# Second feed-forward product issued over 256 weight columns per matmul instead of 512, into the halves of the same accumulator

## The chip, the core and the metric

One core of one Trainium2 chip runs the whole program. Its engines work side by side: TensorE (matmuls, PE in the profile, with its weight loads shown apart as PEld), VectorE (DVE), ScalarE (ACT), GpSimd (POOL) and the queues that issue DMA transfers. The metric is the device time of one execution in microseconds (us); lower is better. A matmul here multiplies a stationary block (loaded first, by an instruction of its own, LDWEIGHTS) with a moving block that streams through the array column by column; the sums land in PSUM, the accumulator memory.

## What is computed

The reference is an attention in two parts followed by a gated feed-forward network:

```python
# q, k, v: (8, 8, 576, 64); factor 4
out_d = sm_attn(mean4(q), mean4(k), mean4(v))      # coarse attention on 144 tokens
out_local = softmax(where(|i - j| < 4, q k / 8)) v # band of 7 neighbours
x = (repeat4(out_d) + out_local) as (4608, 512)
xn = x / sqrt(mean(x * x) + 1e-6) * rms_g
g, val = xn @ w_gate, xn @ w_val                   # (4608, 1536)
out = (g * sigmoid(g) * val) @ w_out               # (4608, 512)
```

## The kernel before

The 4608 tokens are worked on in 18 chunks of 256 tokens (`NCH`, `C`). For every chunk the kernel computes the banded attention on VectorE and ScalarE, adds the coarse attention, normalizes, turns the result with TensorE transposes (line 1080) so that the model dimension lies on partitions, and runs the feed-forward network on TensorE.

Each float32 operand of the two large products is split into a high part and a low part, and each product is made of three: high by high, and high by low in both directions. `Forward.first` (matmul on line 1445) does the first product: for each of 12 slices of 128 hidden units, for gate and for value, 12 matmuls of 128x128 weights as the stationary block with 256 tokens as the moving block, all into one half of a PSUM tile. `Forward.second` (matmul on line 1487) does the second product: for each of the 12 hidden slices `f` and each half `j` of the chunk's tokens, three matmuls with 128x128 hidden activations as the stationary block (`hh`, the high part, twice; `hl`, the low part, once) and 512 columns of `w_out` as the moving block, into the PSUM tile `o[j]` of 128x512, one whole bank. That makes 18 * 12 * 2 * 3 = 1296 matmuls on line 1487.

Between the two, for a pair of slices `n`, ScalarE and VectorE compute the gate: `tanh` (L1453), `gate` (L1457), `product` (L1462), `high` (L1468, writes `hh`) and `low` (L1471, writes `hl`). The second product of a pair runs one pair late (`LAG`), so that TensorE has a first product to do while the gate is computed.

The first three chunks are ordered by a planner (`Plan`) that gives each step an engine, a cost and a due time; it plans one call of `second` (six matmuls) at 1.375 us. From chunk 3 on the loop at the end orders the work: per pair, 24 matmuls of gate and 24 of value (48 on line 1445), then two calls of `second`, with small matmuls of the coarse attention (scores L630, transposes L660, values L675), of the next chunk's mean (L1057) and its transposes (L1080) placed between them. TensorE's order there is fixed by a chain: `in_line` makes each matmul follow the one before it. On the other engines the framework's scheduler chooses the order. When a chunk's twelve slices are summed, `copy` (L740) takes `o[j]` out of PSUM and `store` (L1506) writes it to memory.

Of the kernel before, what the change touches and what calls it, by code (L numbers as in the profile page):

```python
# [27 lines left out]
DM, DF = H * D, 1536  # L28
KT = DM // P
NF = DF // P  # L30
# [200 lines left out]
def attn_moe_kernel(  # L231
# [16 lines left out]
    nc = tc.nc  # L248
# [240 lines left out]
    def heat(out, fresh=True):  # L489

        n = plan.idle
        if spare["open"] and made:
            if "tile" not in spare:
                spare["tile"] = ps_o.tile([P, DM], FP32, name="ps_o")
            out, fresh, n = spare["tile"], True, plan.gap
        n, plan.idle, plan.gap = n * WARM_SHARE, 0.0, 0.0
        cols = 1
        for d in out.shape[1:]:
            cols *= d
        if len(out.shape) > 2:  # L500
            out = out.rearrange({3: "p a b -> p (a b)", 4: "p a b c -> p (a b c)"}[len(out.shape)])
        cols = min(cols, 4 * P) // P * P
        for _ in range(int(n * 2400 / cols) if n > WARM_LEAST and made else 0):
            nc.tensor.matmul(
                out=out[:, :cols], lhsT=one_sb[:, :out.shape[0]], rhs=bcast(zero_sb, 1, cols // zero_sb.shape[1]), start=fresh, stop=fresh,
                skip_group_check=not fresh,
            )
# [6 lines left out]
    def in_line(make):  # L514

        with tc.issue_after(line["last"]) if line["last"] else nullcontext():
            done = make()
        if line["last"]:
            line["last"] = done.ins
        return done  # L520
# [839 lines left out]
    class Forward:  # L1360
# [116 lines left out]
        def second(self, n, i, js=range(2)):  # L1477
            f = 2 * n + i
            if f == 0:
                self.o = [ps_o.tile([P, DM], FP32, name="ps_o") for _ in range(2)]  # L1480
            heat(self.o[0], fresh=f == 0)
            hh, hl = self.hs[n][:, 0, i], self.hs[n][:, 1, i]
            w = [x.part(f // 4)[:, f % 4] for x in wo]
            for j in js:
                cols = slice(j * P, (j + 1) * P)
                for m, (lhs, rhs) in enumerate(((hh, w[0]), (hh, w[1]), (hl, w[0]))):
                    in_line(lambda: nc.tensor.matmul(  # L1487
                        out=self.o[j], lhsT=lhs[:, cols], rhs=rhs,
                        start=(f == 0 and m == 0), stop=(f == NF - 1 and m == 2),
                    ))  # L1490

        def copy(self, j, parts=1):
            if j == 0:
# [16 lines left out]
    for fg in range(3):  # L1510
# [3 lines left out]
        for f in range(4 * fg, 4 * fg + 4, 2 if fg < 2 else 1):  # L1514
            m = 2 if fg < 2 else 1
# [234 lines left out]
```

## Time and profile before

| what | value |
|---|---|
| median of 3 runs | 1086.33 us (1085.03 to 1090.29) |
| span of the profiled execution | 1085.7 us |
| TensorE matmul, busy | 1056.4 us, 97% of the span |
| TensorE weight load, busy | 958.9 us, 88% |
| VectorE, busy | 915.9 us, 84% |
| ScalarE, busy | 598.4 us, 55% |
| GpSimd, busy | 162.0 us, 15% |

The profiled execution lies 0.6 us under the median of the timed runs. Busy time of a matmul includes its way through the array, which overlaps the next matmul; what one matmul costs in a dense stream is therefore read as the distance between the starts of two of them, not as its duration. In a timeline, consecutive instructions of one kind stand in one row with their count.

### The profile page before, as it was taken

How to read it: one execution, taken by the hardware profiler on the slowest of the kernel's cores; microseconds unless marked ns; L12 is line 12 of the kernel's file. 1: busy time of each engine (PE TensorE's matmuls, PEld its weight loads, DVE VectorE, ACT ScalarE, POOL GpSimd, SP SyncE). 2: the span in 40 equal slices, each digit the busy share in tenths (PEclk: the TensorE clock that was granted, in tenths of full speed). 3: DMA queues.
4: the chain of work that ended last, by engine and by line, in shares of the span. 5: the costliest groups of instructions: out<-in, count | busy, mean ns of one | idle time of the engine just before them, and what ended most of it. 6: DMA issues, size and time to landing. Idle time of an engine off the chain costs nothing.

```text
span 1085.7 us, 21625 instructions
## 1 busy us (share of the span) xinstructions
PE 1056.4 (97%) x7983; PEld 958.9 (88%) x7983; DVE 915.9 (84%) x1556; ACT 598.4 (55%) x2029; POOL 162.0 (15%) x200
## 2 busy tenths in 40 slices
PE   6889999999999999999999999999999999999998
PEld 3559899898988999999999999999999989899997
DVE  7789999798969998989898989898989898985322
ACT  5776565737366556565656556565646464554121
POOL 6544654301210000000001000000000000000000
PEclk9899999999999999999999999999999999999999
DMA  9875657323644443434344444442222231300000
GB/s 287 301 216 168 164 142 164 81 80 87 141 98 104 105 129 86 130 85 117 86 99 109 112 98 103 111 103 78 76 73 71 74 96 46 104 17 20 1 20 20
DMA packets 79181, 114.08 MB, mean 105 GB/s; under 512 B 33038, under 2 KB 40406, under 8 KB 79076
## 3 DMA queue, kind: packets, MB, share of 16 engines
q1 hardware_dynamic: 48116, 88.11, 26.5%
q0 software_dynamic: 11680, 19.78, 11.5%
q10 hardware_dynamic: 19280, 4.82, 2.0%
q8 instruction: 62, 1.02, 0.4%
q14 instruction: 43, 0.35, 0.1%
HBM read 100.86 MB, written 11.80 MB: 104 GB/s over the span
## 4 chain that ended last, share of the span: by engine, by line
PE 72%; DVE 6%; ACT 3%; DMA 3%; issue 2%; POOL 0%; SPq 0%; ACTq 0%; DVEq 0%; POOLq 0%
PE ps_h L1445 43%; PE ps_o L1487 22%; PE ps_a L675 2%; ACT prod L1010 2%; DVE x_t L1027 2%; DVE prod L964 1%; DMA qk<-in_qk_sum_dram 1%; PE ps_a L630 1%; PE ps_a L660 1%; PE ps_a L1080 1%; DVE sc L968 1%; DVE prod L1017 1%; DMA kv<-in_k_pad_dram 1%; DVE hs L1471 0%; DVE sil L1462 0%
## 5 line engine op out<-in xcount | busy, mean ns | idle before, releaser
L1445 PE MATMUL ps_h<-xh,w 128*128 128x256 f32 x3456 | 619.9, 279 | 0.1
L1445 PEld LDWEIGHTS ps_h<-xh,w 128*128 128x128 f32 x3456 | 532.3, 188 | 9.0 <-issue 4.5
L1445 PE MATMUL ps_h<-xl,w 128*128 128x256 f32 x1728 | 479.5, 278 | 0.0
L1487 PE MATMUL ps_o<-wo,hs 128*128 128x512 f32 x1296 | 329.3, 396 | 8.4 <-DVE hs L1471 6.2
L1445 PEld LDWEIGHTS ps_h<-xl,w 128*128 128x128 f32 x1728 | 324.9, 188 | 4.3 <-issue 0.6
L1487 PEld LDWEIGHTS ps_o<-wo,hs 128*128 128x128 f32 x1296 | 231.5, 188 | 54.1 <-DVE hs L1471 9.4
L1010 ACT ACTIVATE prod<-kv,sc 128x64 f32<-128x64 f32 x1024 | 263.0, 407 | 25.6 <-DVE sc L1001 8.0
L1468 ACT ACTIVATE hs<-sil 128x512 fp32r<-128x512 f32 x108 | 68.1, 631 | 165.4 <-DVE sil L1462 133.1
L964 DVE TENSOR_TENSOR prod<-q_t,kv 128x896 f32<-128x896 f32 x128 | 138.7, 1104 | 4.6 <-DMA q_t<-in_q_band_dram 3.6
L1027 DVE TENSOR_REDUCE x_t<-prod 128x128 f32<-128x896 f32 x128 | 134.5, 1077 | 3.2 <-ACT prod L1010 3.1
L968 DVE TENSOR_REDUCE sc<-prod 128x14 f32<-128x896 f32 x128 | 135.4, 1075 | 0.2
L1453 ACT ACTIVATE sil<-ps_h 128x512 f32<-128x512 f32 x108 | 64.3, 596 | 125.2 <-PE ps_h L1445 114.6
L1457 DVE SCALAR_TENSOR_TENSOR sil<-sil,ps_h 128x512 f32<-128x512 f32 x108 | 73.6, 682 | 53.9 <-ACT sil L1453 53.1
L1017 DVE TENSOR_TENSOR prod<-sc,kv 128x384 f32<-128x384 f32 (+1 forms) x128 | 106.2, 866 | 0.2
L1462 DVE SCALAR_TENSOR_TENSOR sil<-sil,ps_h 128x512 f32<-128x512 f32 x108 | 73.9, 685 | 35.2 <-PE ps_h L1445 34.9
L1471 DVE TENSOR_TENSOR hs<-sil,hs 128x512 fp32r<-128x512 f32 x102 | 70.1, 688 | 20.1 <-ACT hs L1468 20.0
L417 POOL DMA_DIRECT2D qk<-in_qk_sum_dram x42 | 39.0, 928 | 237.1 <-DMA qk<-in_qk_sum_dram 171.5
L417 POOL DMA_DIRECT2D vs<-in_v_sum_dram x42 | 38.0, 904 | 228.0 <-DMA vs<-in_v_sum_dram 183.4
L650 ACT ACTIVATE a_g<-ps_a,m_g 72x144 f32<-72x144 f32 x128 | 46.5, 371 | 43.0 <-DVE m_g L645 26.2
L1050 ACT ACTIVATE up_t<-x_t 128x128 f32<-128x128 f32 x128 | 39.1, 305 | 11.2 <-DVE x_t L1040 7.0
L675 PEld LDWEIGHTS ps_a<-vs,a_g 72*72 72x72 f32 x512 | 37.9, 145 | 5.4 <-issue 0.8
L740 ACT COPY a_g<-ps_a 72x288 f32<-72x288 f32 x56 | 20.1, 396 | 37.9 <-PE ps_a L660 37.8
(155 smaller groups left out, 815.0 us busy)
## 6 DMA issues: line engine op xcount, KB each, us to landing
kv<-in_k_pad_dram SPq DMA_DIRECT2D x56, 320.0 KB
kv<-in_v_pad_dram SPq DMA_DIRECT2D x56, 320.0 KB
qk<-in_qk_sum_dram POOLq DMA_DIRECT2D x42, 288.0 KB, 4.4
out_dram<-o_sb SPq DMA_DIRECT2D x92, 72.0 KB
vs<-in_v_sum_dram POOLq DMA_DIRECT2D x42, 144.0 KB, 3.9
q_t<-in_q_band_dram SPq DMA_DIRECT2D x150, 36.0 KB
w<-in_w_gate_dram SPq DMA_DIRECT2D x8, 512.0 KB
w<-in_w_val_dram SPq DMA_DIRECT2D x8, 512.0 KB
```

The lines of the kernel that those rows point to most:

```text
L417: nc.gpsimd.dma_start(out=t, in_=(qk_sum, v_sum)[i][self.b, j, :, self.half], accum_op=ALU.add)
L964: nc.vector.tensor_tensor(out=pr, in0=bcast(q[:, s0:s0 + 2], 2, NO), in1=window(k, s0), op=ALU.mult)
L968: nc.vector.tensor_reduce(out=self.sc[:, j, par, s0:s0 + 2], in_=self.pr[i], axis=AX.X, op=ALU.add,)
L1010: nc.scalar.activation(out=self.pr[i][:, o, s], in_=self.v[j, par][:, s0 + s + o], func=AF.Copy, scale=p[:, s, o:o + 1],)
L1017: (nc.vector if engine == "DVE" else nc.gpsimd).tensor_tensor(out=self.pr[i][:, a:b], in0=bcast(p[:, :, a:b].rearrange("p s o -> p o s"), ...
L1027: nc.vector.tensor_reduce(out=self.x[j][:, s0:s0 + 2, par], in_=pr.rearrange("p o s d -> p s d o"), axis=AX.X, op=ALU.add,)
L1445: self.last = nc.tensor.matmul(out=p[n][:, i], lhsT=wi[:, k], rhs=xi[:, k], start=(m == 0), stop=(m == 3 * KT - 1),).ins
L1457: nc.vector.scalar_tensor_tensor(out=self.sil[n], in0=self.sil[n], scalar=1.0, in1=self.g[n], op0=ALU.add, op1=ALU.mult,)
L1462: nc.vector.scalar_tensor_tensor(out=self.sil[n], in0=self.sil[n], scalar=0.5, in1=self.v[n], op0=ALU.mult, op1=ALU.mult,)
L1468: nc.scalar.activation(out=self.hs[n][:, 0], in_=self.sil[n], func=AF.Copy)
L1471: low["last"] = (nc.gpsimd if engine == "POOL" else nc.vector).tensor_tensor(out=self.hs[n][:, 1], in0=self.sil[n], in1=self.hs[n][:, 0], ...
L1487: in_line(lambda: nc.tensor.matmul(out=self.o[j], lhsT=lhs[:, cols], rhs=rhs, start=(f == 0 and m == 0), stop=(f == NF - 1 and m == 2),))
```

## The change

For every hidden slice, token half and product part, the one matmul over 512 columns of `w_out` becomes two over 256 columns each, with the same stationary block, into the left and the right half of the same PSUM tile. Only the first matmul of a chunk's accumulation (`f == 0`, `m == 0`) stays whole. Per chunk 2 of 72 matmuls stay and 70 are split; over 18 chunks 36 stay and 1260 become 2520. The same columns are streamed in all, and the same sums are formed in the same order.

```diff
                 for m, (lhs, rhs) in enumerate(((hh, w[0]), (hh, w[1]), (hl, w[0]))):
-                    in_line(lambda: nc.tensor.matmul(
-                        out=self.o[j], lhsT=lhs[:, cols], rhs=rhs,
-                        start=(f == 0 and m == 0), stop=(f == NF - 1 and m == 2),
-                    ))
+                    parts = 1 if m == 0 and f == 0 else 2
+                    for h in range(parts):
+                        part = slice(h * DM // parts, (h + 1) * DM // parts)
+                        in_line(lambda: nc.tensor.matmul(
+                            out=self.o[j][:, part], lhsT=lhs[:, cols], rhs=rhs[:, part],
+                            start=(f == 0 and m == 0), stop=(f == NF - 1 and m == 2 and h == parts - 1),
+                        ))
```

## Rows read from the trace of the kernel before

**Rows 1.** Page: busy us (share, instructions), granted TensorE clock in 40 slices

```profile
PE 1056.4 (97%) x7983; PEld 958.9 (88%) x7983; DVE 915.9 (84%) x1556; ACT 598.4 (55%) x2029; POOL 162.0 (15%) x200
PEclk9899999999999999999999999999999999999999
```

**Rows 2.** Page: chain that ended last, shares of the span by engine

```profile
PE 72%; DVE 6%; ACT 3%; DMA 3%; issue 2%; POOL 0%; SPq 0%; ACTq 0%; DVEq 0%; POOLq 0%
```

**Rows 3.** Page, costliest groups: busy, mean ns of one, idle before and releaser

```profile
L1487 PE MATMUL ps_o<-wo,hs 128*128 128x512 f32 x1296 | 329.3, 396 | 8.4 <-DVE hs L1471 6.2
```

**Rows 4.** Groups of TensorE matmuls by line, from 360 us to the end

```profile
L1445 PE MATMUL ps_h<-xh,w 128*128 128x256 f32 x2560 | 452.6, 277 | 0.0
L1445 PE MATMUL ps_h<-xl,w 128*128 128x256 f32 x1280 | 354.1, 277 | 0.0
L1487 PE MATMUL ps_o<-wo,hs 128*128 128x512 f32 x972 | 244.4, 395 | 3.6 <-DVE hs L1471 3.6
```

**Rows 5.** Timeline of PE, 600 to 606 us: start us, us, instruction

```profile
600.15 0.28 PE L1445 MATMUL ps_h<-xh,w 128*128 128x256 f32 x1
...
601.30 0.28 PE L1445 MATMUL ps_h<-xl,w 128*128 128x256 f32 x1
...
605.38 0.28 PE L1445 MATMUL ps_h<-xl,w 128*128 128x256 f32 x1
...
605.61 0.62 PE L1487 MATMUL ps_o<-wo,hs 128*128 128x512 f32 x2
```

**Rows 6.** Timeline of PE, 716 to 727 us: a stretch of line 1487

```profile
716.10 2.91 PE L1487 MATMUL ps_o<-wo,hs 128*128 128x512 f32 x12
718.85 1.20 PE L675 MATMUL ps_a<-vs,a_g 72*72 72x64 f32 x16
```

**Rows 7.** Timeline of PEld, 716 to 720 us: the weight loads of that stretch

```profile
715.99 2.59 PEld L1487 LDWEIGHTS ps_o<-wo,hs 128*128 128x128 f32 x12
```

**Rows 8.** Timeline of PE, 847 to 862 us: slow stretch, then quick

```profile
847.66 0.29 PE L1057 MATMUL ps_a<-ss,same_sb 128*128 128x8 f32 x2
...
848.00 0.28 PE L1445 MATMUL ps_h<-xl,w 128*128 128x256 f32 x1
...
853.54 2.96 PE L1487 MATMUL ps_o<-wo,hs 128*128 128x512 f32 x12
856.34 0.28 PE L1445 MATMUL ps_h<-xh,w 128*128 128x256 f32 x1
...
861.80 0.39 PE L1487 MATMUL ps_o<-wo,hs 128*128 128x512 f32 x1
```

**Rows 9.** Timeline of PE, 204 to 222 us: a long slow stretch of line 1445

```profile
204.52 0.28 PE L1445 MATMUL ps_h<-xl,w 128*128 128x256 f32 x1
...
221.84 0.28 PE L1445 MATMUL ps_h<-xl,w 128*128 128x256 f32 x1
```

**Rows 10.** Timeline of PE, 331 to 338 us: line 1445 after line 630

```profile
332.41 0.28 PE L1445 MATMUL ps_h<-xl,w 128*128 128x256 f32 x1
...
337.94 0.40 PE L1487 MATMUL ps_o<-wo,hs 128*128 128x512 f32 x1
```

**Rows 11.** Timeline of PE, 360 to 367 us: line 1445 after line 630

```profile
361.40 0.29 PE L1445 MATMUL ps_h<-xl,w 128*128 128x256 f32 x1
...
366.75 0.62 PE L1487 MATMUL ps_o<-wo,hs 128*128 128x512 f32 x2
```

**Rows 12.** Timeline of PE, 356 to 420 us: small matmuls between

```profile
368.12 1.04 PE L1080 MATMUL ps_a<-ident_sb,x_t 128*128 128x128 f32 x8
...
377.22 0.67 PE L660 MATMUL ps_a<-ident_sb,a_g 72*72 72x72 f32 x8
...
387.37 1.19 PE L675 MATMUL ps_a<-vs,a_g 72*72 72x64 f32 x16
...
404.29 0.66 PE L660 MATMUL ps_a<-ident_sb,a_g 72*72 72x72 f32 x8
...
414.66 1.20 PE L675 MATMUL ps_a<-vs,a_g 72*72 72x64 f32 x16
```

## The prediction

> **What bounds the kernel now.** I read the busy shares first: TensorE is busy for 97% of the span, every other engine for less, and the granted clock is nine tenths or more of the upper level, 2.4 GHz, in every slice of 40 from the third on [rows 1]. In the chain that ended last TensorE has 72%, VectorE 6% [rows 2]. So a nanosecond on TensorE counts nearly in full, unless TensorE was waiting anyway. Does it wait on the changed line? Over the whole run line 1487 had 8.4 us of idle time before it, 6.2 of them for `hl` of VectorE [rows 3]; from 360 us to the end it is 3.6 us, and no other line of TensorE waits there [rows 4]. The change is therefore priced by the pace of TensorE's stream, and the durations of 279 and 396 ns are no help, since they overlap. I take the distance of starts.
>
> **What one piece costs, quick pace.** Line 1445 is what the new matmul looks like: 128x128 stationary, 256 moving columns, into half of a bank, one weight load each. 48 of them run from 600.15 to 605.61, 113.8 ns each; the 36 from 601.30 to 605.38 take 113.3 ns each [rows 5]. The 12 whole ones of line 1487 from 716.10 to 718.85 take 229.2 ns each [rows 6]. Two pieces at 113.3 are 226.7 ns, 2.5 ns less than one whole. From 360 us on there are 972 matmuls on line 1487 [rows 4]; 2 of 72 stay whole, 945 are split: 945 * 2.5 = 2.4 us less.
>
> A smaller term: the 48 of rows 5 cost 5.46 us where 48 at 113.3 would be 5.44. The first few matmuls of line 1445 after line 1487 are slower before they settle. If that comes from the change of length between the two lines, it goes; 3840 matmuls [rows 4] are 80 such stretches of 48, at 0.02 us 1.6 us. I count it in the best case, bound zero to 1.6.
>
> **The additional weight loads.** 1260 are added. TensorE issues one load per matmul, 7983 of each [rows 1], though `hh` is stationary twice running, so none is left out. Before, one load had 229 ns of streaming to hide in; now 113. The load starts 0.11 us ahead of its matmul [rows 6, 7]. Line 1445 has exactly this ratio and keeps 113.3 ns, so I cost the loads at nothing beyond what is in that pace. If they were not covered, the price would be in the pace of the pieces, and that is the next part.
>
> The Trainium skill, "TensorE: Matmul & The Clock Gate", section "Back-to-back issue gap", speaks against the change: a gap of N/2.4 ns plus about 2.5 ns per matmul, so each split would cost 2.5 ns. By that rule 1260 splits would add an estimated 3.2 us. The trace disagrees so far: the pieces of rows 5 are shorter than half a whole one of rows 6, not longer.
>
> **The slow pace.** The same code has a second pace. From 204.52 to 221.84 there are 147 matmuls of line 1445, 117.8 ns each [rows 9]; from 848.00 to 853.54 there are 47 at 117.9, and the 12 whole ones behind them take 233.3 ns each [rows 8]. The granted clock shows no difference between the stages of the one and of the other [rows 1]. So it is 4.4 ns more for 256 columns and 4 ns more for 512; two slow pieces (235.5) cost 2 ns more than one slow whole. The pace sticks: nothing in these 147 steps ends it. It is chosen where the stream starts anew behind other matmuls: behind line 630 it was 117.7 ns once (332.41 to 337.94, 47 steps) [rows 10] and 113.8 another time (361.40 to 366.75) [rows 11]; behind line 1057 it was slow [rows 8]. And it is left at a stretch of line 1487: the 48 matmuls from 856.34 to 861.80 are back at 113.8 [rows 8]. I read the alternation of 512 and 256 columns as what shakes the stream out of the slow pace. The change takes this away: from the first to the second product the step would be the same, and a slow pace could run on until the next other matmul.
>
> From 360 us on there will be 3840 matmuls on line 1445 and 1890 pieces, 5730 steps; all of them slow would cost 5730 * 4.4 = 25 us. How many? In a pattern of some 55 us that repeats, three groups of small matmuls (at 368.12, 377.22, 404.29) stand between two calls of `second`, where 512 columns now follow and soon 256 will; two groups (387.37, 414.66, and then line 630) stand before line 1445 and don't change what follows them [rows 12]. The stretches behind the three are 9.1, 10.2 and, up to 414.66, 10.4 us, 0.54 of the pattern. Behind such groups (lines 660 and 1057) the trace has nine places where 256 columns follow directly; four went slow, one of them shown [rows 8]. So 0.54 * 4/9 = 0.24 of the steps: 6.0 us more. The bounds are none (0 us) and all behind those three, 0.54: 13.5 us.
>
> Before 360 us there are 324 matmuls on line 1487, 315 to be split, in a stage where both paces occur: by 2.5 less or 2 more each that is -0.8 to +0.6 us, and I take zero.
>
> **What hides nothing or stays.** The wait for `hl` comes after two matmuls per `j` as before, with the last piece of `hh` ending some nanoseconds earlier; a shift of this size moves the 3.6 us of waits by no more than their own size. If TensorE becomes quicker, VectorE (84%) is late next, in those same waits. `in_line` fixes TensorE's order, so the pieces stand where the whole stood; nothing is moved past a queue and no wait or DMA is added. `copy` waits for the last piece instead of the last whole. The scheduler may order VectorE's and ScalarE's work differently, since it sees more instructions; its price is bounded by the waits that are there, some 4 us either way.
>
> **Sum.** Quick pieces -2.4, settling -1.6, slow stretches +6.0, early stage 0: +2.0 us. The profiled execution, 1085.7, would be 1087.7; the median lies 0.6 above it, at 1086.3. Forecast 1088.3 us, rounded to 1088.
>
> **Rivals.**
> - All quick. The pieces take the quick pace everywhere after 360 us, as line 1445 mostly does now: -4.0 us, 1082.3. For it: behind line 630 the quick pace returns again and again [rows 11]; against it: rows 8 to 10. Chance 0.25.
> - Slow for long (the other side). Without 512 columns nothing ends the slow pace, and it runs through both products. Slower than 0.5% (5.4 us) means that the slow share passes (5.4 + 4.0)/25 = 0.38; at 0.54 it is -4.0 + 13.5 = +9.5, 1096. Since the pattern repeats, a group that starts slow once may do so in every chunk. Chance 0.20.
> - A fixed cost for each issued matmul, the rule named above. With one half nanosecond more than the quick pace for every piece, 2520 * 0.5 = 1.3 us; with the 2.5 ns of a difference that rows 5 and 6 show, turned the other way, 1260 * 2.5 = 3.2 us, 1089.5. Against it: rows 5. Chance 0.05.
> - Another order on VectorE or ScalarE: waits of line 1487 grow or go, 1083 to 1092. For it: DVE at 84%; against it: TensorE's fixed order. Chance 0.10.
> - That the change doesn't do what it says would show as 1296 matmuls on the line; as every matmul gets its own load now, I see no way to it.
>
> **How the numbers follow.** The mixed case has 0.40, the others 0.25, 0.20, 0.05 and 0.10. The range goes from 1082 (all quick) to 1096 (slow behind all three groups); outside are a still slower pace, an early stage that gains too, and part of the last rival, less than 2 in 10. About 0.5% (5.4 us) is what a measurement of this kernel can tell from no change. Faster by more than that needs all quick and a gain before 360 us as well (0.05) or a better order (0.03): 0.08. Slower by more: the slow rival 0.20, the upper end of the mixed case 0.06, a worse order 0.03: 0.29. The rest, 0.63, is the same.
>
> **What would show it.** Right: 2556 matmuls on line 1487 (36 of 512 columns), pieces at 113 or 118 ns and nothing else, stretches at 118 that begin behind lines 660, 1057 or 1080 and run on through both products. All quick: 113.3 throughout after 360 us, with no settling at the head of line 1445. Wrong: pieces well above 118 ns (loads not covered), idle time before line 1487 well above 4 us after 360 us, or a lower granted clock.

## The result, and the profile after

| | kernel before | changed kernel |
|---|---|---|
| median of the runs | 1086.57 us (1085.03 to 1090.29) | 1095.28 us (1094.03 to 1096.96) |
| span of the profiled execution | 1085.7 us | 1095.2 us |
| ratio after to before | | 1.0072, 95% interval 1.0052 to 1.0091 |

The change makes the kernel slower by 0.72%, more than the 0.5% bound. The page of the changed kernel (busy us, share and instructions of each engine; the chain that ended last; the group of the changed line, now line 1490) answers to [rows 1 to 3]:

```profile
PE 1068.9 (98%) x9243; PEld 1028.3 (94%) x9243; DVE 913.7 (83%) x1556; ACT 597.0 (55%) x2029; POOL 159.7 (15%) x200
...
PE 79%; DVE 9%; ACT 4%; DMA 4%; issue 2%; POOL 1%; SPq 1%; ACTq 0%; DVEq 0%; POOLq 0%
...
L1490 PE MATMUL ps_o<-wo,hs 128*128 128x256 f32 (+1 forms) x2556 | 333.7, 282 | 5.1 <-DVE hs L1471 4.5
```

TensorE's busy time rose from 1056.4 to 1068.9 us and its share of the chain from 72 to 79%; all other engines kept theirs. Idle time before the changed line fell, from 8.4 to 5.1 us. So nothing new is waited for: TensorE's own stream got longer. The groups of its matmuls from 360 us to the end (busy, mean ns of one, idle before) answer to [rows 4]:

```profile
L1445 PE MATMUL ps_h<-xh,w 128*128 128x256 f32 x2560 | 457.9, 279 | 0.0
L1445 PE MATMUL ps_h<-xl,w 128*128 128x256 f32 x1280 | 356.1, 278 | 0.0
L1490 PE MATMUL ps_o<-wo,hs 128*128 128x256 f32 x1933 | 249.3, 281 | 2.8 <-DVE hs L1471 2.7
```

1933 matmuls stand on the changed line where there were 972. But look at line 1445, which the change doesn't touch: its first row went from 452.6 to 457.9 us busy and from 277 to 279 ns, its second from 354.1 to 356.1.

Where the 9.5 us of the profiled executions came in, by the starts of the same matmul of line 1445 in both traces: at the 1297th (351.21 us before, 353.25 after) the distance is 2.0 us; from there to the last one of the 5184 it grows by 7.3 us, evenly, some 0.3 us in every 28; 0.2 us come behind it.

The even growth can be seen in a timeline of PE near the end (start us, us, engine, line, tile, shape, count):

```profile
1059.52 2.88 PE L1490 MATMUL ps_o<-wo,hs 128*128 128x256 f32 x24
1062.24 0.28 PE L1445 MATMUL ps_h<-xh,w 128*128 128x256 f32 x1
...
1067.90 2.99 PE L1490 MATMUL ps_o<-wo,hs 128*128 128x256 f32 x24
1070.73 0.28 PE L1445 MATMUL ps_h<-xh,w 128*128 128x256 f32 x1
```

and further on:

```profile
1076.18 2.88 PE L1490 MATMUL ps_o<-wo,hs 128*128 128x256 f32 x24
1078.90 0.28 PE L1445 MATMUL ps_h<-xh,w 128*128 128x256 f32 x1
...
1084.56 5.70 PE L1490 MATMUL ps_o<-wo,hs 128*128 128x256 f32 x47
```

A piece is one of the two 256-column matmuls that a whole one became. Read the distances between the rows. The 24 pieces from 1059.52 to 1062.24 take 113.3 ns each; the 48 of line 1445 behind them, to 1067.90, 117.9; the next 24 pieces 117.9 (2.83 us); the next 48 of line 1445 113.5 (5.45 us); then pieces at 113.3 (2.72 us) and line 1445 at 117.9 again (5.66 us). Both paces of [rows 5, 8 and 9] are there and nothing else, but here they alternate: slow in line 1445 and the pieces behind it, quick in the next, through both products. In the kernel before, the 48 after such a stretch took 5.46 us [rows 5, 8].

What else differs between a slow and a quick stretch of line 1445 there? Two windows (us, busy time of PE, PEld, DVE, ACT, POOL with counts, granted clock, DMA share, GB/s), the slow one first:

```profile
1062.24:1067.90 5.66, 5.66 (x51) 5.66 (x49) 0.69 (x1) 0.60 (x1) 0.00 (x0) 1.00 0.00 0
1070.73:1076.18 5.45, 5.45 (x50) 5.45 (x49) 0.69 (x1) 0.60 (x1) 0.00 (x0) 1.00 0.00 0
```

Nothing that these views show: the granted clock is 1.00 in both, the DMA share is zero, and VectorE and ScalarE are busy for the same 0.69 and 0.60 us. So the clock and the DMA traffic are out as causes of the slow pace here.

From the starts of all neighbouring matmuls after 360 us (pairs with a wait between them left out) the mean step of line 1445 is 115.26 ns after and 113.86 before; 41% of the steps are at 116 ns or more, where there were 10%. The pieces have 116.34 ns, 65% of them slow; the wholes had 229.38. So line 1445 costs 1.40 * 3818 = 5.3 us more, the changed line (2 * 116.34 - 229.38) * 1815/2 = 3.0 us more, and its waits are 0.8 us less (2.8 us idle after 360 us against 3.6): 7.5 us, where 7.3 are measured. Of the steps at 116 ns or more, the 10% of before are mostly the first few of each stretch; of its 80 stretches of line 1445 after 360 us only 2 are slow as a whole, and 31 in the change.

### The profile page after: what moved, and what is told of

It is laid out like the page before. It is cut to its first block, busy times and chain, and to the rows that moved or that the text cites. A ratio compares the mean times of both kernels' runs of the same rounds, so it can differ in the third digit from the quotient of the medians.

```text
span 1095.2 us, 24157 instructions
## 1 busy us (share of the span) xinstructions
PE 1068.9 (98%) x9243; PEld 1028.3 (94%) x9243; DVE 913.7 (83%) x1556; ACT 597.0 (55%) x2029; POOL 159.7 (15%) x200
## 4 chain that ended last, share of the span: by engine, by line
PE 79%; DVE 9%; ACT 4%; DMA 4%; issue 2%; POOL 1%; SPq 1%; ACTq 0%; DVEq 0%; POOLq 0%
PE ps_h L1445 47%; PE ps_o L1490 24%; ACT prod L1010 3%; PE ps_a L675 2%; DMA w<-in_w_val_dram 1%; DVE prod L964 1%; DVE x_t L1027 1%; PE ps_a L630 1%; PE ps_a L1080 1%; PE ps_a L660 1%; DVE sc L968 1%; DMA kv<-in_k_pad_dram 1%; DMA q_t<-in_q_band_dram 1%; DVE prod L1017 1%; DVE sil L1462 1%
## 5 line engine op out<-in xcount | busy, mean ns | idle before, releaser
L1445 PE MATMUL ps_h<-xh,w 128*128 128x256 f32 x3456 | 627.0, 280 | 0.0
L1490 PE MATMUL ps_o<-wo,hs 128*128 128x256 f32 (+1 forms) x2556 | 333.7, 282 | 5.1 <-DVE hs L1471 4.5
L1490 PEld LDWEIGHTS ps_o<-wo,hs 128*128 128x128 f32 x2556 | 311.8, 188 | 9.3 <-DVE hs L1471 6.0
L675 PE MATMUL ps_a<-vs,a_g 72*72 72x64 f32 x512 | 39.9, 231 | 0.8 <-DVE vs L481 0.4
```

Source lines behind the costliest of these rows:

```text
L1445: self.last = nc.tensor.matmul(out=p[n][:, i], lhsT=wi[:, k], rhs=xi[:, k], start=(m == 0), stop=(m == 3 * KT - 1),).ins
L1490: in_line(lambda: nc.tensor.matmul(out=self.o[j][:, part], lhsT=lhs[:, cols], rhs=rhs[:, part], start=(f == 0 and m == 0), stop=(f == NF - ...
```

## The experiments

The two theories are named as in the expectations. **Load theory**: each split costs something of its own (a load without cover, a fixed cost of a matmul), wherever it stands. **Pace theory**: a piece costs no more than half a whole one; what costs is the slow pace, and line 1445 pays most of it. **Order theory**: another order of the other engines makes TensorE wait. A stretch is a row of matmuls of one line and length; it is called slow when the median of its steps is 116 ns or more (for wholes, above 231 ns). A joint is the place where one stretch follows another. The kernels differ from the one before in the condition that leaves a matmul of line 1487 whole, written `parts = 1 if f == 0 and m == 0 or ... else 2` with the additional condition in place of the dots, unless something else is shown; the diffs stand against the changed kernel's line for `parts`. All times "after 360 us" are from the 1297th to the last matmul of line 1445 in the profiled execution, one for each kernel; steps and stretches are counted from 360 us on, a step under the line that it starts from. Ratios are to the kernel before, timed beside each, with their 95% interval.

| kernel | ratio | splits, of 1260 | after 360 us | step of line 1445, ns | piece, ns | slow stretches of line 1445, of 80 |
|---|---|---|---|---|---|---|
| before | | 0 | 723.9 us | 113.86 | | 2 |
| the change | 1.0072 (1.0052 to 1.0091) | 1260 | 731.2 | 115.26 | 116.34 | 31 |
| late only | 1.0074 (1.0056 to 1.0092) | 980 | 731.1 | 115.26 | 116.36 | 31 |
| early only | 0.9989 (0.9970 to 1.0009) | 280 | 724.4 | 113.95 | | 4 |
| first of a pair whole | 1.0098 (1.0078 to 1.0117) | 1170 | 734.7 | 115.98 | 117.52 | 45 |
| last of a pair whole | 1.0082 (1.0060 to 1.0103) | 1152 | 731.3 | 115.30 | 116.28 | 32 |
| turned order, no split | 1.0000 (0.9986 to 1.0013) | 0 | 724.4 | 113.96 | | 4 |
| turned order, the change | 1.0054 (1.0025 to 1.0083) | 1260 | 731.2 | 115.26 | 116.36 | 31 |
| last of a pair split | 1.0066 (1.0043 to 1.0089) | 108 | 729.3 | 115.21 | 117.89 | 31 |
| by halves | 1.0051 (1.0031 to 1.0070) | 1260 | 731.6 | 115.26 | 116.40 | 31 |
| first call, late | 1.0058 (1.0044 to 1.0072) | 476 | 730.4 | 115.26 | 115.83 | 31 |
| second call, late | 1.0056 (1.0041 to 1.0070) | 504 | 728.4 | 114.84 | 115.76 | 23 |
| early, and first call late | 1.0040 (1.0027 to 1.0054) | 756 | 731.0 | 115.37 | 115.96 | 33 |
| first call of pairs 2 and 5, late | 0.9991 (0.9975 to 1.0007) | 168 | 723.5 | 113.86 | 113.63 | 2 |

**Late only and early only.** The change from chunk 4 on alone, and up to chunk 3 alone.

```diff
-parts = 1 if m == 0 and f == 0 else 2
+parts = 1 if f == 0 and m == 0 or self.c <= FIRST else 2   # late only
+parts = 1 if f == 0 and m == 0 or self.c > FIRST else 2    # early only
```

> The change from chunk 4 on alone; chunks 0 to 3 keep whole matmuls on line 1487. In the profile of the changed kernel the distance to the kernel before grows by 7.3 us from 360 us to the end, steadily, and by 2.0 us before that. Pace theory (line 1445 and the pieces run slow for part of the time, 117.7 instead of 113.3 ns): all of the 7.3 us stays, span about 1093.0 us, slow share on line 1445 after 360 us about 0.4. Order theory (VectorE and ScalarE got another order, by which TensorE waits): the order in chunk 3 is nearly that of before, so most of the loss goes, about 1087 us, with line 1445 after 360 us at its 113.9 ns.

> The change up to chunk 3 alone; from chunk 4 on all are whole. Pace theory: the part after 360 us is as before (line 1445 at 113.9 ns), and what is left is the 2.0 us of before 360 us, span about 1087.7 us. Order theory: the other order of chunk 3 carries the loss, about 1093 us.

Late only, the time after 360 us is that of the change to 0.1 us (731.1 us), with the same mean step of line 1445 (115.26 ns), and the stretch before 360 us lies 0.25 us under before, so the order of the other engines there is out as a cause of the even growth. With waits that became shorter after 360 us, order theory falls for these 7.3 us.

Early only, the time after 360 us is that of before but for 0.5 us. At the 1297th matmul of line 1445 it is not 2.0 us late, as expected, but 1.2 us early (350.00 against 351.21). How much of either belongs to the edit? That stage scatters by as much in kernels whose first chunks are as before. The first matmul of line 1445 starts between 78.4 and 81.9 us in the fourteen profiled executions, ahead of every matmul of the changed line. And first call, late, which runs the same instructions in the same order as before on TensorE, VectorE, ScalarE and GpSimd up to 298 us, reaches the 1297th at 352.96 us, 1.75 us late. Its waits for `hl` from GpSimd, between 80 and 206 us, are longer (us in total, times, longest; before, then first call, late):

```profile
PE ps_o L1487 <- POOL hs L1471: 1.4, 2, 1.0
PE ps_o L1489 <- POOL hs L1471: 3.4, 2, 3.0
```

Two parts of the stage can be told from the scatter. From the 577th to the 865th matmul of line 1445 the five kernels with all matmuls of the first chunks split take 51.4 to 51.6 us and the nine others 52.4 to 52.6: the pieces gain some 1.1 us there. From the 865th to the 1297th the change takes 98.4 us, and the thirteen others 93.9 to 95.0. Two windows of the changed kernel, in the columns of the windows above:

```profile
290.00:311.00 21.00, 19.77 (x171) 18.42 (x172) 13.75 (x31) 11.93 (x49) 3.78 (x5) 1.00 0.56 118
311.00:319.00 8.00, 8.00 (x49) 8.00 (x50) 4.14 (x16) 0.36 (x2) 1.04 (x2) 0.57 0.66 135
```

TensorE was idle for 1.2 us between 290 and 311 us, and in the window behind it the granted clock is 0.57: it stood at the lower level, 1.2 GHz, from 311.5 to 318.3 us. Fifteen steps of line 1445 and two of pieces take 213 ns each there, 0.1 us more than elsewhere: 1.7 us of the loss, with the small matmuls slower beside them. Turned order with the change and by halves have the same splits and no such fall, and 95.0 and 94.0 us in that part; last of a pair whole has a fall of 3.4 us, from 327.3 to 330.7 us. So the 2.0 us of before 360 us are no steady price of the change. That the idle time brought the fall about is not shown: the kernel before is idle for 2.6 us from 319 to 351 us and keeps its clock.

**First or last of a pair whole.** The same number of wholes, at the head or at the end of a pair's twelve.

```diff
-parts = 1 if m == 0 and f == 0 else 2
+parts = 1 if f == 0 and m == 0 or i == 0 and j == 0 and m == 0 else 2   # first whole
+parts = 1 if f == 0 and m == 0 or i == 1 and j == 1 and m == 2 else 2   # last whole
```

> As the change, but the first matmul of each pair's twelve on line 1487 stays whole. Load theory (each split costs the same wherever it stands, 7.3 us / 945 = 7.7 ns after 360 us): 11/12 of the splits, 6.7 us after 360 us, about 1094 us. Pace theory (a whole matmul leaves the stream slow, pieces keep the pace they find, and the step from pieces to line 1445 turns quick to slow and slow to quick): pieces slow (117.7), line 1445 quick after most stretches; also some 7 us, about 1094 us, but with the slow share on line 1445 well under 0.4 and that of the pieces well over 0.64.

> As the change, but the last matmul of each pair's twelve on line 1487 stays whole: as many splits as with the first one whole. Load theory: the same 6.7 us after 360 us, about 1094 us. Pace theory: the pieces are quick, the whole one at the end leaves the stream slow, and the step to line 1445 turns it quick; line 1445 at 113.9 ns as before, pieces mostly at 113.3; after 360 us 1 us less than before, span about 1086.5 us, with 2 us either way for the order in chunk 3.

The load theory gave 6.7 us for both. Measured: 10.9 us with the first one whole, more than the full change with fewer splits, and 7.4 us with the last one. Line 1445 differs between them (115.98 and 115.30 ns), though nothing on it is edited: the load theory can't say that. My own expectations fared no better: with the first whole line 1445 was to be mostly quick and 58% of it is slow; with the last whole all was to be quick and 44% is slow. Timeline of PE with the last one whole (a row with both shapes shows that of its first):

```profile
1043.89 2.88 PE L1489 MATMUL ps_o<-wo,hs 128*128 128x256 f32 x23
1046.61 0.28 PE L1445 MATMUL ps_h<-xh,w 128*128 128x256 f32 x1
...
1052.27 2.98 PE L1489 MATMUL ps_o<-wo,hs 128*128 128x512 f32 x21
1055.09 0.28 PE L1445 MATMUL ps_h<-xh,w 128*128 128x256 f32 x1
```

A whole ends each of the two stretches, just before 1046.61 and 1055.09. The pair from 1043.89 is quick (2.72 us for 22 pieces and a whole) and hands over slow: line 1445 takes 5.66 us from 1046.61 to 1052.27. The next pair is slow. A whole one at the joint does not do what I took it to do. And with the first one whole:

```profile
1037.49 2.99 PE L1489 MATMUL ps_o<-wo,hs 128*128 128x512 f32 x23
1040.31 0.28 PE L1445 MATMUL ps_h<-xh,w 128*128 128x256 f32 x1
...
1045.97 2.99 PE L1489 MATMUL ps_o<-wo,hs 128*128 128x512 f32 x23
```

A pair takes 2.82 us and line 1445 5.66 us: slow throughout in this part, where the change at least alternates. After 360 us the pieces behind the whole at the head of a stretch ran slow in all 81 places; in the change, which has such a whole only at the start of a chunk's sum, in all 13.

**Another order, with and without the change.** On line 1445 the three products of each k in turned order; and, on the changed line, all left halves before the right ones.

```diff
-for wi, xi in ((w[0], self.att.xh), (w[0], self.att.xl), (w[1], self.att.xh)):
+for wi, xi in ((w[1], self.att.xh), (w[0], self.att.xh), (w[0], self.att.xl)):
```

> The kernel before with no split at all; on line 1445 alone the order of the three products of each k is turned (low weights by high input first, then the two others). Same matmuls, loads and columns. Load theory: nothing moves, after 360 us as before, about 1086 us. Pace theory (the pace of 113.3 or 117.7 ns is a state that the stream takes at its joints, whatever the matmuls are): the mean step of line 1445 after 360 us leaves its 113.9 ns; with half of it slow 2.2 ns * 3840 = 8.4 us, about 1094 us; which way the state falls can't be told ahead, so 1085 to 1102 us.

> The change, with the same turned order on line 1445. Load theory: 7.3 us after 360 us over the turned kernel with whole matmuls. Pace theory: another mix of the two paces than in the change (0.41 of line 1445 and 0.65 of the pieces slow there); the difference to the turned kernel with whole matmuls is not 7.3 us, and each kernel's time after 360 us is told by its mean steps.

```diff
-for m, (lhs, rhs) in enumerate(((hh, w[0]), (hh, w[1]), (hl, w[0]))):
-    parts = 1 if m == 0 and f == 0 else 2
-    for h in range(parts):
+for h, (m, (lhs, rhs)) in itertools.product(range(2), enumerate(((hh, w[0]), (hh, w[1]), (hl, w[0])))):
...
```

In this last kernel the whole matmul at the start of a chunk's sum is issued ahead of the pieces of its token half.

> The change with another order of the same pieces: for each token half all pieces of the left half of the columns, then all of the right half, so that the stationary block changes more often. Load theory: each piece costs the same, 7.3 us after 360 us, about 1095 us. Pace theory: another mix of paces; a piece is at 113.3 or 117.7 ns as in the change, line 1445 likewise, and the time after 360 us follows from the two shares, not from the count of pieces.

What I expected of the pace theory fell: the turned order changes nothing. Without splits line 1445 stays at 113.96 ns, with them it is at 115.26 and the pieces at 116.36 ns, where the change has 115.26 and 116.34; by halves likewise (115.26, 116.40). The distance between the two turned kernels after 360 us is 6.8 us, near the 7.3 that the load theory gave. So the mix of paces doesn't hang on which operands follow which, nor on how often the stationary block changes. It goes with the sequence of the stretches: after 360 us, late only and turned order with the change run at the pace of the change in every one of their 203 and 204 stretches of line 1445 and of pieces, though these two ran on different chips, and by halves in 199 of 203. The kernels without splits there agree as well (2, 4 and 4 slow stretches of line 1445, 113.86 to 113.96 ns). This is also why these three can't tell a load cost from a pace; line 1445 does.

**One of twelve split.** The kernel before with only the last matmul of each pair in two pieces.

```diff
-parts = 1 if m == 0 and f == 0 else 2
+parts = 1 if f == 0 and m == 0 or not (i == 1 and j == 1 and m == 2) else 2
```

> The kernel before with only the last matmul of each pair's twelve on line 1487 split: 1 of 12 of the splits. Load theory: 7.3/12 = 0.6 us after 360 us, about 1087 us. Pace theory: what counts is how the stretch hands over to line 1445; if it does as in the change, line 1445 goes from 113.9 to 115.3 ns, 5.4 us, about 1091 us; the wholes on line 1487 stay at 229 ns.

After 360 us it is 5.4 us slower than before: three quarters of the loss with 108 of the 1260 splits. The load theory gave 0.6, the pace theory 5.4. The timeline of PE shows the joint:

```profile
396.01 2.92 PE L1489 MATMUL ps_o<-wo,hs 128*128 128x512 f32 x13
398.77 0.28 PE L1445 MATMUL ps_h<-xh,w 128*128 128x256 f32 x1
...
404.42 1.56 PE L1489 MATMUL ps_o<-wo,hs 128*128 128x512 f32 x6
```

Eleven wholes and two pieces from 396.01 to 398.77 are as quick as twelve wholes (2.76 us; 2.75 in [rows 6]), but line 1445 behind them takes 5.65 us to 404.42, 117.7 ns a step. That happens at 26 of the 58 joints without small matmuls between; in the kernel before at 1 of 58, in the change at 27. The wholes did not stay at 229 ns: their mean is 230.5, and from 1034 us to 1084 us wholes and line 1445 run slow together, though 512 and 256 columns alternate there:

```profile
1065.03 2.96 PE L1489 MATMUL ps_o<-wo,hs 128*128 128x512 f32 x13
1067.83 0.28 PE L1445 MATMUL ps_h<-xh,w 128*128 128x256 f32 x1
...
1073.48 2.96 PE L1489 MATMUL ps_o<-wo,hs 128*128 128x512 f32 x13
```

A pair takes 2.80 us and line 1445 5.65 us.

**One of the two calls split.** From chunk 4 on, the first or the second call of each pair; then the first call with the early part of the change.

```diff
-parts = 1 if m == 0 and f == 0 else 2
+parts = 1 if f == 0 and m == 0 or self.c <= FIRST or i == 1 else 2   # first call
+parts = 1 if f == 0 and m == 0 or self.c <= FIRST or i == 0 else 2   # second call
+parts = 1 if f == 0 and m == 0 or self.c > FIRST and i == 1 else 2   # early, and first call
```

> From chunk 4 on, the first of each pair's two calls on line 1487 is split (as in the change), the second call stays whole: half of the splits after 360 us. Load theory: 7.3/2 = 3.7 us more after 360 us. Pace theory, as the runs so far have it (the joint decides: six wholes ahead of line 1445 hand over quick, as in the kernel before, pieces hand over slow from quick): line 1445 stays at 113.9 ns, the pieces are mostly at 113.3, 945/2 * 2.5 = 1.2 us less after 360 us, span about 1085 us.

> The mirror: from chunk 4 on the second of the two calls is split, the first stays whole; the same number of splits. Load theory: 3.7 us more after 360 us, the same as with the first call. Pace theory: pieces stand ahead of line 1445 as in the change, line 1445 goes to about 115.2 ns, 1.3 * 3840 = 5 us, and the wholes of the first call run at 233 ns behind slow stretches; 5 to 6.5 us more after 360 us, span about 1091 us.

> All of the change up to chunk 3 (1.2 us less at 360 us when it was alone) and the first call from chunk 4 on. Load theory: about 1089 us. Pace theory: both gains together, line 1445 after 360 us at 113.9 ns, span about 1083.5 us, 0.2% under the kernel before.

Again the expectation that six wholes hand over quick fell for a good part of the time: with the first call split it costs 6.5 us, with the second 4.5 (5 to 6.5 expected), against 3.7 for both by the load theory. Line 1445 again carries it (115.26 and 114.84 ns). But with the first call there is a long stretch that does what was expected:

```profile
930.14 2.90 PE L1489 MATMUL ps_o<-wo,hs 128*128 128x256 f32 x18
932.88 0.28 PE L1445 MATMUL ps_h<-xh,w 128*128 128x256 f32 x1
...
938.34 2.90 PE L1489 MATMUL ps_o<-wo,hs 128*128 128x256 f32 x18
941.08 0.28 PE L1445 MATMUL ps_h<-xh,w 128*128 128x256 f32 x1
```

Twelve pieces and six wholes from 930.14 to 932.88 take 2.74 us, line 1445 behind them 5.46 us, and again 2.74: quick throughout, with half of the matmuls split. So it does at 28 of the 58 joints; at the other 30 line 1445 is slow behind the six wholes. In one such place small matmuls stand between the calls:

```profile
435.38 1.64 PE L1489 MATMUL ps_o<-wo,hs 128*128 128x512 f32 x6
436.86 0.28 PE L1445 MATMUL ps_h<-xh,w 128*128 128x256 f32 x1
...
442.51 2.96 PE L1489 MATMUL ps_o<-wo,hs 128*128 128x256 f32 x18
```

Line 1445 takes 5.65 us from 436.86 to 442.51. In the second call's kernel paces alternate in places, as in the change:

```profile
1031.13 2.90 PE L1489 MATMUL ps_o<-wo,hs 128*128 128x512 f32 x18
1033.87 0.28 PE L1445 MATMUL ps_h<-xh,w 128*128 128x256 f32 x1
...
1039.52 2.98 PE L1489 MATMUL ps_o<-wo,hs 128*128 128x512 f32 x18
1042.34 0.28 PE L1445 MATMUL ps_h<-xh,w 128*128 128x256 f32 x1
```

5.65 us from 1033.87 to 1039.52, and the next pair 2.82 us where the quick one had 2.74. The early part of the change beside the first call is 1.2 us early again at the 1297th matmul (350.04 us), but both gains don't come together: 7.1 us are lost after 360 us, and the time is 1.0040 of before.

**Only where the quick stretch was.** From chunk 4 on, the first call of the pairs 2 and 5, in which nothing stands between the two calls.

```diff
-parts = 1 if m == 0 and f == 0 else 2
+parts = 1 if f == 0 and m == 0 or self.c <= FIRST or i == 1 or n not in (2, 5) else 2
```

> From chunk 4 on, the first call on line 1487 is split only in pairs 2 and 5, where no small matmuls stand between the two calls and no matmul of the pair is left whole for the start of the sum; everything else whole. 14 chunks * 2 calls * 6 = 168 splits. Load theory: 168 * 7.7 ns = 1.3 us more after 360 us. Pace theory, by the quick stretches that the kernel with all first calls split had from 923 us on (pieces 113, six wholes 229, line 1445 113): line 1445 stays at 113.9 ns, all pieces at 113.3, 168 * 2.5 ns = 0.4 us less after 360 us; the total the same as before.

This one came out as the pace theory said. After 360 us it takes 723.54 us, 0.32 less than before (0.4 expected; the load theory gave 1.3 more), and the total is the same. The two other kernels without splits there differ from before by 0.5 us, so the 0.32 by itself tells little; the steps tell more. Groups after 360 us, with shapes apart:

```profile
L1445 PE MATMUL ps_h<-xh,w 128*128 128x256 f32 x2560 | 452.6, 277 | 0.0
L1445 PE MATMUL ps_h<-xl,w 128*128 128x256 f32 x1280 | 354.1, 277 | 0.0
L1489 PE MATMUL ps_o<-wo,hs 128*128 128x512 f32 x810 | 207.5, 396 | 3.6 <-DVE hs L1471 3.6
L1489 PE MATMUL ps_o<-wo,hs 128*128 128x256 f32 x324 | 41.4, 276 | 0.0
```

Line 1445 has the 452.6 and 354.1 us of before; 324 pieces have 276 ns, the duration that goes with the quick pace. Timeline of PE:

```profile
1028.36 0.28 PE L1445 MATMUL ps_h<-xh,w 128*128 128x256 f32 x1
...
1033.83 2.90 PE L1489 MATMUL ps_o<-wo,hs 128*128 128x256 f32 x18
1036.56 0.28 PE L1445 MATMUL ps_h<-xh,w 128*128 128x256 f32 x1
...
1042.03 2.22 PE L1489 MATMUL ps_o<-wo,hs 128*128 128x512 f32 x9
```

5.47 us for line 1445, 2.73 us for twelve pieces and six wholes, 5.47 again. Two pieces are 2 * 113.63 = 227.3 ns, a whole is 229.40 in the same kernel.

## Why the prediction was right or wrong

The forecast was 1088 us in a range of 1082 to 1096. The time is 1095.3, inside and near the upper end, and the sign of the sum was right. Its size was not: the sum had +2.0 us where the profiled executions differ by 9.5, 7.3 of them after 360 us; the forecast said no measurable change as the likeliest (0.63), and the kernel is slower by more than 0.5%, which had 0.29.

**What bounds the kernel, and that nothing waits.** Right. TensorE's order held, waits before the line fell a little, VectorE's and ScalarE's busy time stayed.

**The price of a piece.** Right, shown by the last kernel: pieces at 113.6 ns, a pair of them 2.1 ns less than a whole one (2.5 forecast). The additional loads cost nothing beyond it. Where both lengths ran at the quick pace, two pieces took 227.3 ns and a whole one 229.4. The Trainium skill, "TensorE: Matmul & The Clock Gate", section "Back-to-back issue gap", gives the formula that the prediction cites as that of an isolated matmul; by it each split would be an estimated 2.5 ns dearer. No run here bears that out for this stream.

**The settling.** Of the 1.6 us little came: quick stretches of line 1445 behind pieces take 5.45 us, behind wholes 5.46.

**The slow pace.** That there are two paces, and that the slow one decides, was right: 4.4 ns a step, paid on an unchanged line for 5.3 of the 7.3 us. The term that failed is its share. I put it at 0.24 of the 5730 steps. Measured, 0.31 more of the steps of line 1445 are slow than before (0.41 against 0.10) and 0.65 of the pieces, together 0.42. With that, 25 * 0.42 less 2.4 for the quick pieces and 0.8 for the waits gives 7.3 us.

**Why the share was too small.** Two readings failed. The first is that the alternation of 512 and 256 columns ends the slow pace. Last of a pair split keeps the alternation and runs slow through six pairs on end. The trace of before has it too, behind the stretch of [rows 9]:

```profile
228.43 1.56 PE L1487 MATMUL ps_o<-wo,hs 128*128 128x512 f32 x6
229.83 0.28 PE L1445 MATMUL ps_h<-xh,w 128*128 128x256 f32 x1
...
231.24 1.56 PE L1487 MATMUL ps_o<-wo,hs 128*128 128x512 f32 x6
232.63 0.28 PE L1445 MATMUL ps_h<-xh,w 128*128 128x256 f32 x1
```

Six wholes take 1.40 us and the twelve of line 1445 behind them 1.41, 117.5 ns each: the slow pace passes through both lengths.

The second reading is that slow stretches begin only behind groups of small matmuls. Some do in the change:

```profile
379.25 0.66 PE L660 MATMUL ps_a<-ident_sb,a_g 72*72 72x72 f32 x8
379.71 1.66 PE L1490 MATMUL ps_o<-wo,hs 128*128 128x256 f32 x12
381.21 0.28 PE L1445 MATMUL ps_h<-xh,w 128*128 128x256 f32 x1
...
386.86 2.99 PE L1490 MATMUL ps_o<-wo,hs 128*128 128x256 f32 x24
389.69 1.20 PE L675 MATMUL ps_a<-vs,a_g 72*72 72x64 f32 x16
```

Line 1445 takes 5.65 us from 381.21 and the 24 pieces behind it 2.83. Counted over the matmuls of both lines after 360 us, 0.48 are in slow stretches. Of these, 0.16 are in runs that began behind the three groups which the sum counted at 0.24: the pieces were slow behind line 1080 in 13 of 13 places, behind line 660 alone in 9 of 9, behind lines 660 and 1057 in 0 of 8, where the sum took 4 of 9 for all. In the last chunks 0.09 began behind line 1057 where it stands before line 1445, a place that the sum left out. A further 0.18 are in runs that began at the joint from quick pieces to line 1445, which is followed by slow matmuls in all 14 places, with no small matmul between; and 0.05 began behind the whole that opens a chunk's sum. From slow pieces to line 1445 the pace turned quick at 31 of 44 joints. From line 1445 to pieces directly behind it, the pace stayed as it was at all 67. The rows for the joint and the whole couldn't be had from the trace of before, in which line 1445 never follows 256 columns of line 1487; the bound of 0.54 covered the share, the value taken did not.

**Before 360 us.** The term of zero, with bounds of -0.8 and +0.6 us, was wrong both ways: the pieces gained some 1.1 us between 204 and 257 us, where 204 matmuls of line 1445 that were slow in before [rows 9] ran quick. The profiled execution lost more than that to a stretch at the lower clock, which two kernels with the same splits did not have.

**The rivals.** "Slow for long" is what happened in size, with an added share of 0.42 where its threshold was 0.38; its picture of a pace that nothing ends was wrong, since 31 of 44 joints from slow pieces to line 1445 end it. "All quick" fell with 31 slow stretches of line 1445 for 2. The fixed cost fell (one of twelve splits made three quarters of the loss; 168 of them in another place cost none). The other order fell for the time after 360 us (late only, and shorter waits).

**What stays open.** What the two paces are, and by which rule a joint picks one. Shown is that the pace doesn't belong to the matmul, since unchanged ones run in both; that the order of the operands has no influence on it; and that the same sequence of stretches gives the same paces, place by place, in other executions and on different chips. Not separated is what in the sequence counts: a split changes the lengths and also the number of matmuls and loads ahead of a joint, and no run changed one without the other. Three rules that I made from the traces for which way it falls (a whole at the end, a turned order, six wholes behind pieces) failed when they were tried; only a copy of a stretch that had been seen quick held. Other lengths than 256 and 512 were not tried.

## What to carry to other kernels

Price a matmul by the distance of starts in a dense stretch, and look whether that distance has more than one value before taking its mean; here 4.4 ns on some thousand steps were the whole loss. An edit of the matmuls in one loop can change the pace of the unchanged loop behind it, so compare the step of every line of the engine, not only that of the edited one. When such a state decides, test an edit by moving it within the stretch with its count kept: a cost that belongs to the instruction stays, one that belongs to the joint moves.

## What the runs showed of the hardware

A dense stream of float32r matmuls with 128x128 stationary blocks and 256 columns ran at 113.3 ns or at 117.7 ns a step, at the same granted clock of 1.00 and without DMA traffic in the two windows compared, and stayed at either through 204 matmuls on end; 512 columns ran at 229 or 233 ns. Splitting 512 columns into two loads and two matmuls was not dearer in the quick pace (227.3 against 229.4 ns). Two pieces in place of one whole ahead of a joint turned the 48 matmuls behind it slow (5.46 to 5.65 us) at 26 of 58 joints, where 1 of 58 was slow before. The same sequence of stretches took the same pace at 203 of 203 and 204 of 204 places in two executions on different chips. And the clock fell to its lower level for 6.8 us in the middle of one profiled execution and for 3.4 us in another, out of fourteen; 256 columns took 213 ns there.
